# Up-projections of two batches cut into quarters, gates into halves, and a new order table: attention followed by a gated channel mix on one core

## The chip, the cores and the metric

The kernel runs on one core of one Trainium2 chip. The metric is device microseconds for one execution of the whole program. The engines are TensorE (PE), VectorE (DVE), ScalarE (ACT), GpSimd (POOL) and SyncE (SP, which here only issues DMAs).

## The reference

Eight batches, eight heads, 576 positions, head size 64. A linear attention without a big score matrix feeds a channel mix:

```
q_s = softmax(q, over d);  k_s = softmax(k, over positions)
kv  = k_s^T v                     # 64x64 per head
x   = q_s kv                      # joined over heads: (8, 576, 512)
xp  = x shifted by one position (0 in front)
xk  = mu_k*x + (1-mu_k)*xp;  xr = mu_r*x + (1-mu_r)*xp
k   = relu(xk @ w_k)              # 512 -> 1024
out = sigmoid(xr @ w_r) * ((k*k) @ w_v)
```

Inputs and output are float32 in HBM; the products run in bf16.

## The kernel before

**Units.** A batch is handled in two units u of four heads. Position 9p+j of a batch sits on partition p of block j, so that a batch has nine blocks of 64 rows, and "shifted by one" is the block before. Two batches make a pair i, with nine output tiles m of 128 rows.

**Steps of a unit.** load q, k, v (SyncE); exp of q and of k (ScalarE, L332); cast_v to bf16 (L336); sum_q and scale_q on VectorE (L341, L346); q is turned, for batches 0 and 1 by TensorE (turn_q, L357, and evict_q), later by a DMA (dma_turn_q, L368); kv (36 small 64x64 products, L372). Then the batches part:

- Batches 0 and 1 (NM = 2) fold the mix into the weights: weigh_kv (VectorE, L388) makes four scaled copies of kv, and x_mixed (L398) makes xk (w=0) and xr (w=1) directly, in two column parts c (blocks 0 to 4 and 5 to 8, PARTS). So x_mixed(b,u,w,c) has 12 matmuls for c=0 and 8 for c=1. evict_mixed copies each to SBUF.
- Batches 2 to 7 make x (L424), then shift_x (ScalarE, L438) and mix_x (VectorE, L443) blend each row half h for w=0 and w=1.

**Steps of the mix.** up(b,f) (L450) makes 128 of the 1024 hidden units, eight matmuls: two column halves a by four groups ct of 128 channels. Channels 2u and 2u+1 come from unit u. relu (ScalarE), square of two f at once (VectorE or ScalarE). gate(i,m) (L471): four matmuls over ct, then tanh. down(i,m) (L487): eight matmuls, finish (VectorE, L494), store.

**Weights** come as float32 into buffers that the run needs later, and are cast once: w_k in two halves of four f (load_wk; cast_wk, eight steps on GpSimd, ScalarE or VectorE), w_r (two casts on GpSimd), w_v (load_wv in two halves into the place where w_k lay; four casts).

**PSUM.** Three tiles of two banks ("two": turn, kv, x, x_mixed, up) and two of one bank ("one": gate, down).

**Order.** All of it is a list of steps. The class Plan takes a table ORDER of step numbers; a letter behind a number names the engine where there is a choice (A ScalarE, D VectorE, G GpSimd). It works out a start time for each step from costs written in the code, hands out buffers by it and emits the steps in order of these start times. On each engine the instructions stand in the table's order, and each engine takes its own strictly in that order; SyncE's loads, turns and stores likewise. TensorE's first fifteen microseconds are filled up with idle products (warm).

At the end, a branch (part) chooses a general path when a check of the softmax sums fails; then only the last two downs, finishes and stores follow.

Of the kernel before, what the change touches and what calls it, by code (L numbers as in the profile page):

```python
# [21 lines left out]
7 0 2 8 1 76 3 80 81 4 9 10 96 11 5 100 78G 77 79A 82 85 83A 12 6 13 84A 97 14 101 86 87 28 102  # L22
103A 90 92 91A 104D 93A 98G 99G 19 105 94 95A 16G 88 17G 106 107 108 89A 27 109D 24 110 111A 29
23G 136 15A 114 18D 112 362 363 21G 115D 367 30 113D 31 365 360 22G 25 32 368 26 33 372 20A 37
34 40 366 361 377 375 140 141 116 378 364D 376 370 120 371 369D 121 142 119G 526 536 117 527
143D 138G 122 42 373 118D 537 39G 144D 124D 125 43 137 521 531 123D 139A 44 38G 126 127 130 131A
128 129A 145 146 147 134 41 135A 148 149A 532 150 151D 36G 374A 152 154 153D 385 387 155D 35D
386 382 397 522 379D 156 159 388 523 398 160 389A 158 524 528 380 173 176 177 174 46 161 529 383
381 45 157 390 391 178 530 538 190 539 395 162 132 533 396 163 399A 392 133A 164 393 561 193 166
534 165 384D 47 49 394D 562 541 48 175 167 168 542 169 179 55 180 551 50 546 194 195 552 535 181  # L30
170 547 186 187 172 171 188 182 51 563 183 564 548 556 184 207 412 413 191 192 185 210 417 189
402 418 403 415 410 540 211 241 565 405 209 416 549 411 407 212 208 419D 408 406 244 245 576 196
197 400 56 57 557 571 401 414D 577 213 198 409D 572 200 404D 214 558 199 202 203 201 543 215 559
544 204 206 205 52 216 581 566 582 217 219 53 54 567 220 221 224 218 225 525 222 227 223 568 578
427 432 428 242 550 569 430 243 431 433 420 421 247 226 230 434A 586 246 437 228 248 438 587 579
422 423 58 231 249 254 255 424D 256 59 229 570 583 250 257 560 251 584 545 553 258 253 232 554
61 237 66 252 234 573 574 233 591 64 238 425 606 236 60 426 259 235 63 239 260 435 240 277 261
65 607 452 436 442 447 439D 429D 596 453 262 592 443 440 575 448 275 445 294 450 292 446 278 608
62 279 580 441 295 449D 451 597 293 263 455 264 280 298 598 444A 454A 609 601 299 456 276 265
599 266 600 602 267 268 281 282 270 555 611 612 67 588 269 68 272 621 283 589 271 274 622 273  # L40
285 284 593 73 289 594 69 626 286 610 288 627 457 616 458 603 459A 296 290 287 343 309 460 74
291 467 461 468 462 463 346 465 311 470 472 466 297 312 477 310 313 471 344 75 604 469D 590 628
478 345 473 300 585 314 617 347 71 315 618 302 595 629 316 641 301 305 619 304 464A 306 475 308
646 642 647 630 613 476 307 303 348 474A 317 323 479D 322 349 614 350 620 636 637 319 638 643
324 318 320 485 321 487 488 72 328 644 651 325 652 486 70 497 639 640 498 489D 492 326 329 490
493 327 495 496 482 483 330 491 499D 623 351 332 357 624 661 353 615 653 333 480 356 662 331
494D 481 358 654 352 656 657 631 632 359 484D 334 625 633 340 335 336 355 673 655 339 634 648
337 354 341 517 342 518 338 505 649 666 510 645 650 667 704 671 506 705 511 672 507 681 674 706
707 682 512 635 500 508 509A 513 515 675 676 514D 658 659 677 516 502 501 503 504D 660 519D 668
669 605 670 663 664 665 683 684 678 679 691 685 686 692 696 687 688 697 680 708 520 689 690 701  # L50
702 693 694 703 695 698 699 700
# [3 lines left out]
class Plan:  # L55
# [7 lines left out]
    TURN = 0.2  # L63
# [7 lines left out]
    def step(self, eng, cost, fn=None, after=(), uses=(), lat=0.12, narrow=False):  # L71
        s = {"eng": eng if isinstance(eng, dict) else {eng: cost}, "fn": fn, "lat": lat,
             "n": len(self.steps), "prev": [], "uses": [], "tail": False, "narrow": narrow}
        self.steps.append(s)
        self.link(s, after, uses)
        return s
# [7 lines left out]
    def run(self):  # L84

        busy, narrow, order = {e: 0.0 for e in ENGINES}, False, []
        for word in ORDER.split():
# [24 lines left out]
        return sorted(order, key=lambda s: s["start"])  # L112
# [30 lines left out]
def kernel(  # L143
# [18 lines left out]
    J = S // 64  # L162
# [123 lines left out]
    def wk_raw():  # L286
        return f32(at("k2", "w"), CT * F).rearrange("p (c a f) -> p a c f", a=2, c=CT)
# [162 lines left out]
    def up(b, f):  # L450
        ps, xk = at("two", "up", b, f), at("xk", b)
        for a in range(2):
            for ct in range(CT):
                nc.tensor.matmul(ps[:, a, 0:HS], lhsT=wk_bf[:, ct, 128 * f:128 * f + 128],  # L454
                                 rhs=xk[:, ct, HS * a:HS * a + HS], start=(ct == 0),
                                 stop=(ct == CT - 1))
# [14 lines left out]
    def gate(i, m):  # L471
        for ct in range(CT):
# [66 lines left out]
    T_UP, T_GATE, T_DOWN, T_NARROW = 0.98, 0.863, 1.725, 0.5  # L539
# [30 lines left out]
    for a in range(2):  # L570
        queue.append(dma(2.85, lambda a=a: load_wk(a), after=early[-1:], uses=[sl("k2", "w")]))
        for c in range(4):
            ev["wk", 4 * a + c] = pl.step(
                {"POOL": 0.65, "ACT": 0.58, "DVE": 0.6}, 0,
                lambda e, f=4 * a + c: cast_wk(e, f), after=[queue[-1]], uses=[sl("k2", "w")])
    queue.append(dma(2.85, load_wr, after=early[-1:], uses=[sl("xr", "w")]))
    ev["wr"] = [pl.step("POOL", 1.05, lambda c=c: cast_wr("POOL", c), after=[queue[-1]],
                        uses=[sl("xr", "w")]) for c in range(2)]
# [3 lines left out]
    for a in range(2):  # L582
        first.append(dma(2.75, lambda a=a: load_wv(a), uses=[sl("k2", "w")],
                         after=[*queue, *(ev["wk", i] for i in range(FT))]))
        for c in (2 * a, 2 * a + 1):
            ev["wv"].append(pl.step({"POOL": 1.2, "ACT": 1.05, "DVE": 0.9}, 0,
                                    lambda e, c=c: cast_wv(e, c), after=[first[-1]],
                                    uses=[sl("k2", "w")]))
# [4 lines left out]

    for n in range(B):
        for u in range(2):
# [5 lines left out]
            if n < NM:  # L601
# [3 lines left out]
                                     ev["ld", "v", n, u]], uses=[vb, sl("ldv", n, u)])  # L605
                      for h in range(2)]
            else:
                vc = [pl.step("POOL", 1.3, lambda n=n, u=u: cast_v("POOL", n, u),
                              after=[ev["ld", "v", n, u]], uses=[vb, sl("ldv", n, u)])]
            p = pl.step("DVE", 1.57, lambda n=n, u=u: sum_q(n, u), after=[qe], uses=[eq])  # L610
            p = pl.step("DVE", 1.32, lambda n=n, u=u: scale_q(n, u), after=[p], uses=[eq, qs])
# [13 lines left out]
            if n < NM:  # L625
                km = sl("kvm", n, u)
                nk = [p, ev["mu"]]
                for w in range(2):
                    nk.append(pl.step("DVE", 0.75 - 0.2 * w, lambda n=n, u=u, w=w: weigh_kv(n, u, w),
                                      after=nk, uses=[s, km, sl("mub")], lat=0.18))  # L630
                for w in range(2):
                    for c in range(2):
                        s = sl("two", "xm", n, u, w, c)
                        p = pl.step("PE", 0.47 if c == 0 else 0.41,
                                    lambda n=n, u=u, w=w, c=c: x_mixed(n, u, w, c),
                                    after=[nk[2 + w], *T], uses=[qT, km, s], lat=0.3, narrow=True)
# [6 lines left out]
            nk = pl.step("DVE", 0.42, lambda n=n, u=u: norm_kv(n, u), after=[p], uses=[s, kn],  # L643
                         lat=0.35)
            ss = [sl("two", "x", n, u, h) for h in range(2)]
            p = pl.step("PE", T_NARROW, lambda n=n, u=u: x(n, u), after=[nk, *T],
# [13 lines left out]
    for b in range(B):  # L660
        mixed = [ev["mix", b, u, 0, c] for u in range(2) for c in range(2)]
        relus = []
        for f in range(FT):
            s, r = sl("two", "up", b, f), sl("rel", b, f // 2)
            ev["up", b, f] = pl.step("PE", T_UP, lambda b=b, f=f: up(b, f),
                                     after=[ev["wk", f], *mixed], uses=[sl("xk", b), s], lat=0.2)
            relus.append(pl.step("ACT", 0.54, lambda b=b, f=f: relu(b, f),
                                 after=[ev["up", b, f]], uses=[s, r], lat=0.2))
            if f % 2:
# [3 lines left out]
                                              lat=0.2)  # L673
                relus = []
    for s in (ev["prep"], ev["up", 0, 0]):
        pl.link(s, [], [sl("one", "warm")])
    branch = pl.step("PE", 0.3, lambda: part())
    branch["tail"] = "first"
    for i in range(B // 2):
        for m in range(J):  # L680
            bs = [b for b in (2 * i, 2 * i + 1) if (m <= 4 if b == 2 * i else m >= 4)]
            s, th, ot = sl("one", "rp", i, m), sl("th", i, m), sl(kept(i, m), i, m)
            p = pl.step("PE", T_GATE, lambda i=i, m=m: gate(i, m),
                        after=[*ev["wr"], *(ev["mix", b, u, 1, c] for b in bs for u in range(2)
                                            for c in range(2))],
                        uses=[sl("xr", i), s, th], lat=0.2)
# [146 lines left out]
```

## Time and profile before

| | |
|---|---|
| median of 3 runs | 199.39 us (198.61 to 199.65) |
| the profiled execution | 199.28 us, span in the profile 197.5 us |
| granted TensorE clock, mean | 0.989 |
| busy: PE, DVE, ACT, POOL | 186.5, 145.6, 144.7, 30.4 us |
| read from and written to HBM | 33.56 and 9.44 MB |

A line of a timeline reads: start in us, length in us, engine, line of the kernel, operation, output <- input by tile names, shape, how many instructions the line merges, and in brackets the idle time just before it and what ended it. "PE two L454 <- POOL wk_bf L238: 0.9, 1, 0.9" in the list of waits: instructions of line 454 waited for a GpSimd cast of wk_bf, 0.9 us in total, once, longest 0.9. L238 and L237 are the copy helper (VectorE or GpSimd, and ScalarE). The busy digits are tenths in 40 equal slices of the span.

### The profile page before, as it was taken

How to read it: one execution, taken by the hardware profiler on the slowest of the kernel's cores; microseconds unless marked ns; L12 is line 12 of the kernel's file. 1: busy time of each engine (PE TensorE's matmuls, PEld its weight loads, DVE VectorE, ACT ScalarE, POOL GpSimd, SP SyncE). 2: the span in 40 equal slices, each digit the busy share in tenths (PEclk: the TensorE clock that was granted, in tenths of full speed). 3: DMA queues.
4: the chain of work that ended last, by engine and by line, in shares of the span. 5: the costliest groups of instructions: out<-in, count | busy, mean ns of one | idle time of the engine just before them, and what ended most of it. 6: DMA issues, size and time to landing. Idle time of an engine off the chain costs nothing. (4 is left out here: it accounts for less than half of the span.)

```text
span 197.5 us, 4726 instructions
## 1 busy us (share of the span) xinstructions
PE 186.5 (94%) x1903; PEld 111.4 (56%) x1903; DVE 145.6 (74%) x225; ACT 144.7 (73%) x212; POOL 30.4 (15%) x42
## 2 busy tenths in 40 slices
PE   6699899899999999999998999999999999999991
PEld 4366665655547754664675545755476546664441
DVE  1979896797899799948999779887658859126222
ACT  3898688799797986989769988998749591671210
POOL 2042763420120222000080000230200000000000
PEclk9879999999999999999999999999999999999998
DMA  5999999989999999869993499999622540515634
GB/s 207 371 399 386 389 390 386 389 314 240 276 388 205 229 397 294 272 61 278 403 399 87 86 250 359 318 229 276 236 51 59 113 106 10 124 30 124 162 72 127
DMA packets 35896, 46.86 MB, mean 237 GB/s; under 512 B 16280, under 2 KB 16544, under 8 KB 35872
## 3 DMA queue, kind: packets, MB, share of 16 engines
q1 hardware_dynamic: 35456, 46.02, 77.7%
q10 hardware_dynamic: 416, 0.53, 1.0%
q8 instruction: 15, 0.25, 0.5%
q14 instruction: 9, 0.07, 0.1%
HBM read 33.56 MB, written 9.44 MB: 218 GB/s over the span
## 5 line engine op out<-in xcount | busy, mean ns | idle before, releaser
L454 PE MATMUL two<-xk,wk_bf 128*128 128x288 bf16 x512 | 66.8, 286 | 1.2 <-POOL wk_bf L238 0.9
L490 PE MATMUL one<-wv_bf,k 128*128 128x512 bf16 (+1 forms) x296 | 66.2, 374 | 0.1
L454 PEld LDWEIGHTS <-wk_bf 128*128 128x128 bf16 x512 | 49.8, 98 | 18.1 <-POOL wk_bf L238 1.2
L459 ACT ACTIVATE rel<-two 128x576 bf16<-128x576 f32 x64 | 39.9, 650 | 20.3 <-PE two L454 17.0
L490 PEld LDWEIGHTS <-k 128*128 128x128 bf16 x296 | 28.1, 98 | 31.2 <-issue 0.8
L473 PE MATMUL one<-wr_bf,xr 128*128 128x512 bf16 x144 | 35.8, 379 | 0.0
L238 POOL CAST vb<-ldv 128x1152 bf16<-128x1152 f32 (+1 forms) x17 | 19.2, 1132 | 102.0 <-DMA ldv<-in_v_dram 94.0
L440 ACT ACTIVATE aw<-two,om 128x575 bf16<-128x575 f32 x48 | 32.6, 752 | 2.5 <-PE two L432 2.5
L478 ACT ACTIVATE th<-one 128x512 f32<-128x512 f32 x36 | 21.4, 603 | 13.5 <-PE one L473 13.4
L496 DVE SCALAR_TENSOR_TENSOR ot<-th,one 128x512 f32<-128x512 f32 x33 | 22.4, 681 | 11.9 <-PE one L490 9.1
L469 DVE TENSOR_TENSOR k<-rel 128x1152 bf16<-128x1152 bf16 x22 | 18.6, 860 | 11.3 <-ACT rel L459 11.2
L342 DVE TENSOR_REDUCE rs<-eq 128x18 f32<-128x1152 bf16 x16 | 21.6, 1348 | 3.4 <-ACT eq L332 3.3
L347 DVE TENSOR_TENSOR qs<-eq,inv 128x1152 bf16<-128x1152 bf16 x16 | 23.7, 1484 | 0.3
L445 DVE SCALAR_TENSOR_TENSOR xk<-two,mu,aw 128x576 bf16<-128x576 f32 x24 | 19.1, 812 | 3.3 <-ACT aw L440 3.3
L332 ACT ACTIVATE eq<-ldq 128x1152 bf16<-128x1152 f32 x16 | 18.5, 1170 | 3.2 <-DMA ldq<-in_q_dram 3.0
L473 PEld LDWEIGHTS <-xr 128*128 128x128 bf16 x144 | 13.4, 98 | 13.1 <-issue 0.2
L445 DVE SCALAR_TENSOR_TENSOR xr<-two,mu,aw 128x576 bf16<-128x576 f32 x24 | 19.1, 803 | 1.1 <-ACT aw L440 1.0
L332 ACT ACTIVATE ek<-ldk 128x1152 bf16<-128x1152 f32 x16 | 18.7, 1171 | 0.5 <-DMA ldk<-in_k_dram 0.5
L467 ACT ACTIVATE k<-rel 128x1152 bf16<-128x1152 bf16 x10 | 11.6, 1171 | 0.2
L378 PE MATMUL two<-vb,ek 64*64 64x65 bf16 x576 | 7.9, 197 | 1.0 <-ACT ek L332 0.5
L378 PEld LDWEIGHTS <-ek 64*64 64x64 bf16 x576 | 6.4, 110 | 3.9 <-ACT ek L332 0.9
L320 PE MATMUL one<-ident 128*128 128x256 bf16 x29 | 6.6, 387 | 1.8 <-DVE halves L258 1.8
(56 smaller groups left out, 86.0 us busy)
## 6 DMA issues: line engine op xcount, KB each, us to landing
ldq<-in_q_dram SPq DMA_DIRECT2D x16, 576.0 KB, 5.9
ldk<-in_k_dram SPq DMA_DIRECT2D x16, 576.0 KB, 8.4
out_dram<-ot SPq DMA_DIRECT2D x66, 128.0 KB, 2.5
ldv<-in_v_dram SPq DMA_DIRECT2D x14, 576.0 KB, 7.7
k<-in_moe_w_k_dram SPq DMA_DIRECT2D x2, 1024.0 KB, 12.6
k<-in_moe_w_v_dram SPq DMA_DIRECT2D x2, 1024.0 KB, 11.0
ldv<-in_v_dram SPq DMA_DIRECT2D x4, 288.0 KB, 10.5
xr<-in_moe_w_r_dram SPq DMA_DIRECT2D x1, 1024.0 KB, 13.1
```

What stands on the lines that cost most here:

```text
L238: return {"DVE": nc.vector, "POOL": nc.gpsimd}[eng].tensor_copy(out=out, in_=in_)
L332: nc.scalar.activation(out=at("e" + n, b, u)[:].rearrange("p j (h d) -> p h j d", h=2), in_=at("ld" + n, b, u)[:].rearrange("p h (j d) -> ...
L342: nc.vector.reduce_sum(out=rs[:], in_=at("eq", b, u)[:].rearrange("p j (h d) -> p (j h) d", h=2), axis=AX.X)
L347: nc.vector.tensor_tensor(out=at("qs", b, u)[:].rearrange("p j (h d) -> p (j h) d", h=2), in0=at("eq", b, u)[:].rearrange("p j (h d) -> p ...
L440: nc.scalar.activation(out=at("aw", b, u, h, w)[:, 1:S], in_=x_of(b, u, h)[:, 1:S], func=ACT.Copy, scale=om[:, c:c + 1])
L445: nc.vector.scalar_tensor_tensor(out=blend(b, w)[:, 2 * u + h, :], in0=x_of(b, u, h)[:, 64:64 + S], scalar=mu[:, c:c + 1], in1=at("aw", b, ...
L454: nc.tensor.matmul(ps[:, a, 0:HS], lhsT=wk_bf[:, ct, 128 * f:128 * f + 128], rhs=xk[:, ct, HS * a:HS * a + HS], start=(ct == 0), stop=(ct ...
L459: nc.scalar.activation(out=at("rel", b, f // 2)[:, f % 2, :].rearrange("p (a c) -> p a c", a=2), in_=at("two", "up", b, f)[:, :, 0:HS], fu ...
L473: nc.tensor.matmul(at("one", "rp", i, m)[:], lhsT=at("xr", i)[:, ct, 128 * m:128 * m + 128], rhs=wr_bf[:, ct, :], start=(ct == 0), stop=(c ...
L478: nc.scalar.activation(out=at("th", i, m)[:], in_=at("one", "rp", i, m)[:], func=ACT.Tanh, scale=0.5)
L490: nc.tensor.matmul(at("one", "vp", i, m, a)[:, cols], lhsT=at("k2", i)[:, f, 128 * m:128 * m + 128], rhs=wv_bf[:, f, cols], start=(f == 0) ...
L496: nc.vector.scalar_tensor_tensor(out=at(kept(i, m), i, m)[:, cols], in0=at("th", i, m)[:, cols], scalar=1.0, in1=at("one", "vp", i, m, a)[ ...
```

## The change

up gets the column halves and the units that it is to do, and gate the units:

```diff
-    def up(b, f):
+    def up(b, f, parts=(0, 1), us=(0, 1)):
         ps, xk = at("two", "up", b, f), at("xk", b)
-        for a in range(2):
-            for ct in range(CT):
+        for a in parts:
+            for ct in range(2 * us[0], 2 * us[-1] + 2):
...
-    def gate(i, m):
-        for ct in range(CT):
+    def gate(i, m, us=(0, 1)):
+        for ct in range(2 * us[0], 2 * us[-1] + 2):
```

In batches 0 and 1 an up becomes four steps, (a,u) for a and u in 0, 1, of two matmuls each; the quarter of u=0 opens the sum and that of u=1 closes it. A quarter of u=0 can run before unit 1's xk is there. Gates of pair 0 with m >= 4 become two steps by unit. The float32 place of w_k is laid out so that each half is contiguous:

```diff
-        return f32(at("k2", "w"), CT * F).rearrange("p (c a f) -> p a c f", a=2, c=CT)
+        return f32(at("k2", "w"), CT * F).rearrange("p (a c f) -> p a c f", a=2, c=CT)
```

The plan's clockwork learns that some steps of VectorE and GpSimd hold each other up (casts, scale_q, squares), and some costs are new:

```diff
-    TURN = 0.2
+    TURN, SHARE = 0.25, 0.7
...
+            if s["shares"] and e in sharing:
+                a, b = sharing["POOL" if e == "DVE" else "DVE"]
+                cost += self.SHARE * max(0.0, min(b, t + cost) - max(a, t))
+                sharing[e] = t, t + cost
...
-    T_UP, T_GATE, T_DOWN, T_NARROW = 0.98, 0.863, 1.725, 0.5
+    T_UP, T_GATE, T_DOWN, T_NARROW = 0.98, 0.863, 1.725, 0.55
...
-                    p = pl.step("PE", 0.47 if c == 0 else 0.41,
+                    p = pl.step("PE", 0.65 if c == 0 else 0.52,
```

These numbers act only through the emission's order. The number of matmuls, copies, loads and stores is the same. The table ORDER is new throughout. Read out of it, by step names:

```
TensorE, batch 0, before
  x_mixed(0,0,*) kv(0,1) x_mixed(0,1,*), all eight | up 1 3 2 0 | up 5 7 6 4 | turn_q(1,1) | gate 1 3
  turn_q(1,0) kv(1,0) gate 0 2
after
  six x_mixed and kv(0,1) | quarters of up 1 0 3 2 | x_mixed(0,1,1,0) x_mixed(0,1,1,1)
  quarters of up 4 5 6 7, turn_q(1,1) inside the last | gate 1 3 | turn_q(1,0) kv(1,0) gate 0 2
TensorE, batch 1, before
  seven x_mixed and kv(1,1) | up 2 3 1 7 | down 0 1 | up 0 4 | down 3 | up 6 | kv(2,0) x_mixed(1,0,1,0)
  down 2 | up 5 | x(2,0) gate 8 4 kv(2,1) gate 6 5 x(2,1) down 8 5 gate 7 | ups of batch 2
after
  six x_mixed and kv(1,1) | quarters of up 4 7 5 6 0 2 1 3 | down 3 1 | x_mixed(1,1,1,0) kv(2,0)
  x_mixed(1,1,1,1) | down 0 2 | x(2,0) kv(2,1) halves of gate 8 4 5 6 x(2,1) down 8 5 | gate 7 | ups of batch 2
cast_wk   before: GpSimd 1 2 7 5 6, ScalarE 0 4, VectorE 3
          after:  GpSimd 1 7 5, VectorE 0 3 2 4 6
cast_wr   both: GpSimd; the halves 0 1 before, 1 0 after
evict_mixed of batch 1   before: ScalarE 5, VectorE 3; after: ScalarE 8
between the last x of batch b and its first up, before
  b=3 gate gate down down | b=4 down gate up gate up | b=5 down gate up gate down | b=6 kv gate down down
after
  b=3 kv gate down down   | b=4 gate down up gate    | b=5 down up down gate      | b=6 down down gate
```

The last steps on TensorE are down(3,6), the branch, and then, before, down(3,8) first half, down(3,7), down(3,8) second half; after, down(3,7), down(3,8) in two halves.

More of the change, by code (lines that the diff above doesn't have):

```diff
@@ L28 @@
[L28 to L33, printed above, removed]
@@ new lines @@
+14 87 104A 28 88 16G 89D 103A 19 23G 94 95A 105 90 91A 27 106 92 93A 108 107 109A 110 111A 15D
+18D 365 24 367 366 360 21G 378 29 361 26 136 17D 368 379 369 362 376 377 373 363 380 374 364 140
+371 372 20D 30 22D 112 25 31 114 375 382 33 115A 383 384 119G 385 113D 387 393 389 395 139G 388
+116 386 390 396 394 32 391 141 398 37 399 370A 117 397 142 120 138G 121 400 144D 401 574 402
+143D 584 585 575 122 118D 125 569 123A 579 137 124D 126 127 580 128 145 146 147 134 129A 135A
+132 133A 148 149A 130 392D 131A 150 426 427 151A 442 443 34 444 445 40 381A 35D 446 431 433 428
@@ new lines @@
+192 454 56 464 599 196 625 212 197 583 629 630 213 462D 198 467D 592 200 214 199 455 201 610 243
+593 202 203 204 206 205 53 456 611 242 457D 634 215 247 245 635 248 216 619 217 218 221 620 58
+220 621 222 600 631 223 52 224 468 469 612 225 478 219 227 228 54 226 470 246 632 479 471 472D
+258 475 476 480 481 639 640 230 249 65 254 255 622 644 229 231 473 474 256 250 633 645 251 60
+482D 257 594 604 252 293 66 485 636 623 253 486 232 238 605 659 637 626 237 59 660 261 234 233
+239 61 483 484 477A 240 654 235 236 495 496 627 259 262 490 487D 649 275 650 491 62 488 493 489
@@ new lines @@
+317 322 323 324 318 319 676 326 677 696 699 320 538 325 321 539 543 347 545 700 697 546 540 530
+541 678 544 668 709 710 348 542D 531 329 330 533 704 705 528 529 689 690 691 331 534 692 351 357
+332 352 356 706 547D 693 333 707 532A 358 535 714 359 536 715 724 673 353 334 537D 716 717 725
+355 339 340 711 718 712 336 341 701 726 354 335 337 563 564 338 558 702 553 559 554 555 713 708
+556 565 727 342 757 728 758 759 550 566 557A 567A 719 734 698 735 760 720 548 551 560 549 729
+552D 561 562D 721 703 722 730 723 736 737 731 686 732 738 739 687 733 744 740 749 745 741 750
@@ L69, in slot, with step @@
         return {"kind": kind, "users": 0, "idx": None, "end": 0.0}
-    def step(self, eng, cost, fn=None, after=(), uses=(), lat=0.12, narrow=False):
+    def step(self, eng, cost, fn=None, after=(), uses=(), lat=0.12, narrow=False, shares=False):
         s = {"eng": eng if isinstance(eng, dict) else {eng: cost}, "fn": fn, "lat": lat,
-             "n": len(self.steps), "prev": [], "uses": [], "tail": False, "narrow": narrow}
+             "n": len(self.steps), "prev": [], "uses": [], "tail": False, "narrow": narrow, "shares": shares}
         self.steps.append(s)
@@ L86, in run @@
         busy, narrow, order = {e: 0.0 for e in ENGINES}, False, []
+        sharing = {"DVE": (0.0, 0.0), "POOL": (0.0, 0.0)}
         for word in ORDER.split():
@@ L574 @@
                 {"POOL": 0.65, "ACT": 0.58, "DVE": 0.6}, 0,
-                lambda e, f=4 * a + c: cast_wk(e, f), after=[queue[-1]], uses=[sl("k2", "w")])
+                lambda e, f=4 * a + c: cast_wk(e, f), after=[queue[-1]], uses=[sl("k2", "w")],
+                shares=True)
     queue.append(dma(2.85, load_wr, after=early[-1:], uses=[sl("xr", "w")]))
     ev["wr"] = [pl.step("POOL", 1.05, lambda c=c: cast_wr("POOL", c), after=[queue[-1]],
-                        uses=[sl("xr", "w")]) for c in range(2)]
+                        uses=[sl("xr", "w")], shares=True) for c in range(2)]
     first = [ld(n, 1, u, early[-1:]) for n, u in (("q", 0), ("q", 1), ("k", 0), ("v", 0), ("k", 1))]
@@ L592 @@
                 ld(n, b, u, first)
+    weighed: list = []
     for n in range(B):
@@ L608 @@
                 vc = [pl.step("POOL", 1.3, lambda n=n, u=u: cast_v("POOL", n, u),
-                              after=[ev["ld", "v", n, u]], uses=[vb, sl("ldv", n, u)])]
+                              after=[ev["ld", "v", n, u]], uses=[vb, sl("ldv", n, u)],
+                              shares=True)]
             p = pl.step("DVE", 1.57, lambda n=n, u=u: sum_q(n, u), after=[qe], uses=[eq])
-            p = pl.step("DVE", 1.32, lambda n=n, u=u: scale_q(n, u), after=[p], uses=[eq, qs])
+            p = pl.step("DVE", 1.32, lambda n=n, u=u: scale_q(n, u), after=[p], uses=[eq, qs],
+                        shares=True)
             if n < NM:
@@ L633 @@
                         s = sl("two", "xm", n, u, w, c)
-                        p = pl.step("PE", 0.47 if c == 0 else 0.41,
+                        p = pl.step("PE", 0.65 if c == 0 else 0.52,
                                     lambda n=n, u=u, w=w, c=c: x_mixed(n, u, w, c),
-                                    after=[nk[2 + w], *T], uses=[qT, km, s], lat=0.3, narrow=True)
+                                    after=[nk[2 + w], *T], uses=[qT, km, s], lat=0.25, narrow=True)
                         ev["mix", n, u, w, c] = pl.step(
@@ L642 @@
             kn = sl("kvs", n, u)
-            nk = pl.step("DVE", 0.42, lambda n=n, u=u: norm_kv(n, u), after=[p], uses=[s, kn],
-                         lat=0.35)
+            nk = pl.step("DVE", 0.42, lambda n=n, u=u: norm_kv(n, u), after=[p],
+                         uses=[s, kn], lat=0.35)
             ss = [sl("two", "x", n, u, h) for h in range(2)]
-            p = pl.step("PE", T_NARROW, lambda n=n, u=u: x(n, u), after=[nk, *T],
+            p = pl.step("PE", T_NARROW, lambda n=n, u=u: x(n, u), after=[nk, *T, *weighed],
                         uses=[qT, kn, *ss], lat=0.3, narrow=True)
@@ L660 @@
     for b in range(B):
-        mixed = [ev["mix", b, u, 0, c] for u in range(2) for c in range(2)]
         relus = []
         for f in range(FT):
-            s, r = sl("two", "up", b, f), sl("rel", b, f // 2)
-            ev["up", b, f] = pl.step("PE", T_UP, lambda b=b, f=f: up(b, f),
-                                     after=[ev["wk", f], *mixed], uses=[sl("xk", b), s], lat=0.2)
+            s, r, both = sl("two", "up", b, f), sl("rel", b, f // 2), []
+            whole = ((0, 1), (0, 1), 0.2)
+            for a, us, lat in (whole,) if b >= NM else [
+                    ((a,), (u,), 0.2 * u) for a in range(2) for u in range(2)]:
+                ev["up", b, f] = pl.step(
+                    "PE", T_UP * len(a) * len(us) / 4,
+                    lambda b=b, f=f, a=a, us=us: up(b, f, a, us),
+                    after=[ev["wk", f], *(ev["mix", b, u, 0, c] for u in us for c in range(2)
+                                          if c in a or c == 0 or b >= NM),
+                           *(both[-1:] if us == (1,) else ())],
+                    uses=[sl("xk", b), s], lat=lat)
+                both.append(ev["up", b, f])
             relus.append(pl.step("ACT", 0.54, lambda b=b, f=f: relu(b, f),
-                                 after=[ev["up", b, f]], uses=[s, r], lat=0.2))
+                                 after=both, uses=[s, r], lat=0.2))
             if f % 2:
@@ L676, with needs @@
         pl.link(s, [], [sl("one", "warm")])
+    def needs(b, m, c):
+        lo, n = PARTS[c]
+        return b >= NM or any(lo <= blk - J * (b % 2) < lo + n for blk in (2 * m, 2 * m + 1))
     branch = pl.step("PE", 0.3, lambda: part())
@@ L682 @@
             s, th, ot = sl("one", "rp", i, m), sl("th", i, m), sl(kept(i, m), i, m)
[L683 to L686, printed above, removed]
+            p = None
+            for us in ((0, 1),) if i or m < 4 else ((0,), (1,)):
+                p = pl.step("PE", T_GATE * len(us) / 2, lambda i=i, m=m, us=us: gate(i, m, us),
+                            after=[*ev["wr"], *(ev["mix", b, u, 1, c] for b in bs for u in us
+                                                for c in range(2) if needs(b, m, c)),
+                                   *([p] if p else ())],
+                            uses=[sl("xr", i), s, th], lat=0.2 if us[-1] else 0.0)
             t = pl.step("ACT", 0.49, lambda i=i, m=m: tanh(i, m), after=[p], uses=[s, th],
```

46 lines of the change are left out of this document (19 added, 27 removed).

## The prediction

> **What bounds the kernel now.** I read the page first, then the waits of TensorE, then the timeline of the two stretches that the change rewrites (16 to 40 us, and the ups that open each later batch), and last the chain that ends the run.
>
> ```profile
> span 197.5 us, 4726 instructions
> PE 186.5 (94%) x1903; PEld 111.4 (56%) x1903; DVE 145.6 (74%) x225; ACT 144.7 (73%) x212; POOL 30.4 (15%) x42
> ...
> PE   6699899899999999999998999999999999999991
> ...
> GB/s 207 371 399 386 389 390 386 389 314 240 276 388 205 229 397 294 272 61 278 403 399 87 86 250 359 318 229 276 236 51 59 113 106 10 124 30 124 162 72 127
> ```
>
> A slice is 4.94 us. From the ninth slice to the last but one TensorE is full; DMA moves 371 to 399 GB/s in the second to eighth slice. So there are two regimes: up to 40 us bytes are owed, after that TensorE's own work is the time. What TensorE waited for:
>
> ```profile
> PE two L361 <- DVE qs L347: 1.5, 1, 1.5
> PE two L454 <- POOL wk_bf L238: 0.9, 1, 0.9
> PE two L378 <- ACT ek L332: 0.5, 1, 0.5
> PE two L410 <- ACT xk L237: 0.4, 2, 0.3
> ```
>
> Only the third lies behind 40 us. An edit of order can win the few waits of the head, that 0.5, and no more; the end (last down at 193.45, finish, store, 4.05 us) is the same work in both tables. The stretch with the largest wait that the change touches:
>
> ```profile
> 17.56 2.62 PE L454 MATMUL two<-xk,wk_bf 128*128 128x288 bf16 x20
> ...
> 20.19 3.41 POOL L238 CAST wk_bf<-k 128x512 bf16<-128x512 f32 x3 [3.02 <-DMA k<-in_moe_w_k_dram]
> ...
> 20.37 1.64 DVE L347 TENSOR_TENSOR qs<-eq,inv 128x1152 bf16<-128x1152 bf16 x1
> ...
> 22.54 4.09 PE L454 MATMUL two<-xk,wk_bf 128*128 128x288 bf16 x32 [0.89 <-POOL wk_bf L238]
> ...
> 24.43 2.55 POOL L238 CAST wr_bf<-xr 128x1024 bf16<-128x1024 f32 x2 [0.83 <-DMA xr<-in_moe_w_r_dram]
> ...
> 26.98 1.89 PE L473 MATMUL one<-wr_bf,xr 128*128 128x512 bf16 x8
> ```
>
> Four ups run on the first half of w_k, then TensorE stands 0.89 us for GpSimd's casts of the second half. The first gate begins at 26.98, the moment wr's cast ends (24.43 + 2.55).
>
> **Part 1, batch 0 (16 to 29 us).** The change splits an up into four quarters of two matmuls: the same 8 matmuls in all, 4.09/32 = 0.128 us each, nothing added. It puts two of the mixed products (20 matmuls, about 0.8 us by the starts 16.31 to 17.16 to 17.56) behind the first four ups, and gives VectorE five of the eight w_k casts (before: one), ScalarE none (before: two). The first half's cast of f=1 is there at 16.6 (16.00 + 0.61), and the quarters of unit 0 need only unit 0's evictions, so ups start about 16.7 rather than 17.56. Four ups, 4.05, give 20.75; the two products 21.55. The second half lands at 20.19; casts of 0.61 (GpSimd) and 0.43 (VectorE), one after the other 7, 4, 5, 6, end at 20.8, 21.2, 21.8 and 22.2; up 4 wants its cast at 21.55, ups 5 and 6 at 22.6. The 0.89 wait is covered. Four ups and turn_q (0.6) end at 26.2, against 26.98 with the same work done.
>
> What is late next: wr. Its landing (24.43) is bound by bytes and moves with nothing here; two casts of 1.04 alone end at 26.5, so gates start 0.45 earlier at most. And behind them kv(1,0) needs a half of v that VectorE casts last: scale_q(1,0) after the lock 26.5 to 27.85, two evictions 0.42 each, cast 0.66: 29.35, so kv(1,0) at 29.4, where before it ran at 29.45. The gain of this part, 0.45 to 0.8, is given back there: I take 0, and keep 0 to 0.45.
>
> The casts are put one after the other because GpSimd's and VectorE's shared steps exclude each other in the rows: a w_k cast takes 613 ns alone and 1738 ns beside scale_q,
>
> ```profile
> L238 POOL CAST wk_bf<-k x5: 613/613/1738, 16.0 to 22.4; 128x512 bf16<-128x512 f32 x5
> ```
>
> and wr's second cast took 1.56 instead of 1.04 behind a square. The 1738 ns cast was queued at 20.8 and ran when scale_q ended at 22.01: it stood still for the rest of it, and did not run slower. The Trainium skill, SBUF — State Buffer, section "SBUF: two separate sides", speaks against the change here: the port pair that the two engines share is an exclusive lock, held for a whole instruction by whichever came first. The trace agrees (1.13 us of standing still). By that rule a scale_q(1,0) that starts just ahead of wr's second cast would hold all gates back by its whole 1.34 us, and the total below would be -0.3; if the two only slowed each other, as 1.56 for 1.04 might be read, it would stay -1.1. Whose turn comes first is rival 2.
>
> The new layout of w_k's raw half (contiguous per half) frees load_wv from the other half's casts: SyncE's 2.7 us wait there (issue at 23.63) shrinks to about 22.2. The queue in front was not empty (388 GB/s between 16 and 27), so 0, at most nothing gained or lost.
>
> **Part 2, batch 1 (29.4 to 40 us).** Before, seven mixed products and kv run from 31.70 to 35.29 with small waits (0.42, 0.43, 0.27, 0.34 in the loads' and matmuls' rows), and the first up starts at 35.64. After, six products stand ahead of the ups instead of seven. All six evictions are on ScalarE, start to start 0.59 and 0.48: first at 32.15, the fourth done at 34.45, which frees the two-bank tile of up 4: ups from 34.55. That is 1.1 earlier, less one product (0.45) still owed: 0.65. ScalarE then owes a square 1.07, eight relus 0.53, four exps 1.07, a tanh 0.48 up to 45.7; the ups need their tiles at 40.45 (relu 0 done 39.7) and 40.9 (relu 6 done 40.25): no wait, with 0.65 to spare. Take -0.65; ends 0 (ScalarE's ops at full duration, 0.1 more each, use the spare) and -1.65 (gates at 26.5 and no wait until the fourth up).
>
> **Part 3, the rest.** kv(6,0) waited 0.51 at 108.60 for its exp; the table puts that exp some 15 ScalarE steps earlier: -0.5 (ends 0 and -0.5). A narrow step (64-row products) between wide ones costs more than one beside another narrow one: kv and x alone take 0.41 + 0.40 (starts 53.50 to 53.91, 51.27 to 51.67), together 0.69 (70.65 to 71.34), and the up ahead of one 1.07 against 0.98. Behind 40 us the new order has 15 such groups for 17: 0.1 to 0.2 each, -0.3. Halved gates add no instruction. New waits in 150 us of other order: before had one of 0.5; bounds 0 and 1.0, I take +0.35.
>
> Sum: -0.65 - 0.5 - 0.3 + 0.35 = **-1.1 us**. The profiled execution took 199.28 us (span 197.5 and 1.78 around it): 198.2; it stood 0.11 under the median of 199.39: 198.3.
>
> **Rivals.** (1) *Bytes hold the head*: part 2's lead is lost to v and k of batch 1 as part 1's is to wr. For it: 388 GB/s up to 40 us. Against: the waits of 31.7 to 35.6 name evictions, not DMA. Then -0.45, 198.9. (2) *The lock falls the other way*: scale_q(1,0) starts before 25.42 and wr's second cast waits 1.34. Gates at 27.85, kv(1,0) at 30.2 instead of 29.45: -1.1 + 0.8, 199.1. I have the scale ready at 25.85, 0.4 on the good side. (3) *Slower: the blends of batches 3 to 6 come late.* The first up of a batch waits for the last xk blend on VectorE. Before, it had little to spare:
>
> ```profile
> 79.47 0.82 DVE L445 SCALAR_TENSOR_TENSOR xk<-two,mu,aw 128x576 bf16<-128x576 f32 x1 [0.21 <-ACT aw L440]
> ...
> 80.56 1.63 PE L454 MATMUL two<-xk,wk_bf 128*128 128x288 bf16 x12
> ```
>
> 80.29 against 80.56: 0.27, and by the same reading 0.6, 0.8 and 0.5 in batches 4 to 6. TensorE's work between the batch's last x and its first up (gate 0.87, down 1.73, up 0.98, kv 0.4) shrinks from 5.2, 5.43, 6.18, 4.73 to 4.73, 4.45, 5.31, 4.33: by 0.47, 0.98, 0.87, 0.40. If blends come as long after x as before: waits of 0.2, 0.4, 0.1, 0 = 0.7. If each comes 0.5 later (one tanh ahead on ScalarE): 0.70 + 0.88 + 0.57 + 0.40 = 2.55, and the time is 199.39 - 1.45 + 2.55 = 200.5. It makes the kernel slower from some 0.2 later on, where these waits reach 1.45. Against it: the new order puts both xk blends of the last unit ahead of an xr one in most of these batches. (4) *The split gives nothing and nothing else moves*: quarters are worth no time where ups wait for casts and tiles, as in part 1; inside 198.9 to 199.4.
>
> **How the numbers follow.** Half a per cent, 1.0 us, is about what a measurement of this kernel can tell (its three runs span 1.04). Forecast 0.56, of which 0.44 is over 0.5% faster; rivals 1 and 4 0.16, nearly all within; rival 2 0.09, of which 0.05 within (what is later behind it decides); rival 3 0.16, slower; 0.03 for a full win of all waits (-1.65 - 0.5 - 0.4 = -2.5, 196.9). Faster 0.47, same 0.33, slower 0.20. The range runs from that full win, 196.9, to rival 3's 200.5; the forecast's own is 197.3 to 199.0.
>
> **What would show it.** Right: no wait of an up on wk_bf; gates first at 26.5 to 27.0; batch 1's first up at 34.3 to 34.9; kv(6,0) unwaited; TensorE's last down at about 192.4. Wrong: the first gate later than 27.5 (rival 2); batch 1's ups at 35.5 (rival 1); waits of L454 on VectorE's L445 behind 70 us (rival 3).

## The result and the profile after

The changed kernel takes 198.68 us (median of 22 runs, 196.69 to 199.88), the kernel before 199.60 in the same series (22 runs, 198.61 to 200.60). The ratio is 0.9946, 95% interval 0.9925 to 0.9966: about 1.1 us faster. Runs that took over 1.5% more than the fastest of the same kernel are left out of this ratio and of those below: one here, one of after_again, two of scale_late. The profiled execution took 198.17 us with a span of 196.3, before 199.28 and 197.5. The total came out as forecast, but its parts did not.

The page of the changed kernel, span, busy times and TensorE's slices:

```profile
span 196.3 us, 4719 instructions
...
PE 186.9 (95%) x1904; PEld 111.7 (57%) x1904; DVE 143.6 (73%) x224; ACT 145.6 (74%) x214; POOL 30.1 (15%) x41
...
PE   6989969999999999999999999999999999999992
```

TensorE's busy time is the same within 0.4 us (186.9, before 186.5); its idle time fell from 11.0 to 9.4 us. Its waits, in the order engine, tile and line that waited, what it waited for, total, times, longest:

```profile
PE one L481 <- POOL wr_bf L246: 1.6, 1, 1.6
PE two L369 <- DVE qs L355: 0.7, 1, 0.7
PE two L418 <- ACT xk L245: 0.3, 1, 0.3
PE one L498 <- DVE ot L504: 0.3, 1, 0.3
PE two L462 <- ACT xk L245: 0.2, 1, 0.2
```

(Lines have moved by 8 to 10: up L462, gate L481, down L498, kv L386, scale_q L355, the copy helper L246 and L245.) The waits on wk_bf and on the exp of k(6,0) are gone, as forecast. A new one of 1.6 us, the largest in the part that the change rewrites, stands ahead of the first gate. The timeline shows how it came about:

```profile
16.75 4.09 PE L462 MATMUL two<-xk,wk_bf 128*128 128x288 bf16 x32
...
20.38 1.18 DVE L246 CAST wk_bf<-k 128x512 bf16<-128x512 f32 x2
20.41 1.62 POOL L246 CAST wk_bf<-k 128x512 bf16<-128x512 f32 x2 [3.73 <-DMA k<-in_moe_w_k_dram]
...
22.21 1.34 DVE L355 TENSOR_TENSOR qs<-eq,inv 128x1152 bf16<-128x1152 bf16 x1
...
23.47 1.34 DVE L350 TENSOR_REDUCE rs<-eq 128x18 f32<-128x1152 bf16 x1
...
24.61 3.15 POOL L246 CAST wr_bf<-xr 128x1024 bf16<-128x1024 f32 x2 [2.58 <-DMA xr<-in_moe_w_r_dram]
...
25.14 1.71 DVE L355 TENSOR_TENSOR qs<-eq,inv 128x1152 bf16<-128x1152 bf16 x1
...
27.81 1.89 PE L481 MATMUL one<-wr_bf,xr 128*128 128x512 bf16 x8 [1.64 <-POOL wr_bf L246]
...
35.56 8.00 PE L462 MATMUL two<-xk,wk_bf 128*128 128x288 bf16 x64 [0.18 <-ACT xk L245]
```

TensorE begins its ups at 16.75 and is ready for the gates at about 26.2. But scale_q(1,0) on VectorE starts at 25.14, while w_r's first cast runs on GpSimd, and gets its turn before the second one. The two casts, 1.04 us each alone, take 3.15, and the first gate runs at 27.81. Batch 1's first up comes at 35.56, before 35.64: nothing is won by then. The gain lies later. From 100 to 125 us (columns: window, length, busy time of PE, PEld, DVE, ACT, POOL, granted clock, DMA share, GB/s), the kernel before and then the one after:

```profile
100.00:125.00 25.00, 24.36 (x264) 14.08 (x263) 21.71 (x29) 21.90 (x31) 3.92 (x4) 1.00 0.77 238
```

```profile
100.00:125.00 25.00, 25.00 (x277) 15.39 (x276) 20.83 (x30) 19.66 (x30) 3.53 (x2) 1.00 0.96 282
```

The starts of single steps, read off TensorE's weight loads (a few matmul records are missing, loads hardly ever), cut the span into three. "Last" is down(3,8) second half; "body" reaches from batch 2's first up to it, "tail" from there to the span's end. (after_again and late_again are experiments below.)

| kernel | up(0) | kv(1,0) | up(1) | up(2) | body | tail | span |
|---|---|---|---|---|---|---|---|
| before | 17.55 | 29.36 | 35.23 | 60.26 | 131.92 | 5.30 | 197.48 |
| after | 16.75 | 30.12 | 35.31 | 60.57 | 130.71 | 5.00 | 196.28 |
| after_again | 16.70 | 31.48 | 37.14 | 62.07 | 130.70 | 5.01 | 197.78 |
| late_again | 17.70 | 29.60 | 34.82 | 59.74 | 130.70 | 5.04 | 195.48 |

So the change is +0.31 in the head, -1.22 in the body and -0.30 in the tail: -1.21. The head differs from execution to execution of the same kernel. The body of the new table hardly does; the old table's was 131.92 here and 132.37 in before_tail (below), where the exp of k(6,0) held TensorE 0.9 us instead of 0.5.

What TensorE did in the body (columns as above), before and then after:

```profile
60.26:192.18 131.92, 131.13 (x1215) 76.65 (x1214) 96.12 (x140) 95.23 (x142) 12.15 (x9) 1.00 0.71 195
```

```profile
60.57:191.28 130.71, 130.56 (x1216) 76.59 (x1215) 95.35 (x143) 93.98 (x140) 13.22 (x10) 1.00 0.74 205
```

So of the 1.22, 0.64 is idle time (0.79 before, 0.15 after) and 0.57 is busy time, for the same matmuls.

### The profile page after: what moved, and what is told of

The parts are those of the page before. It is cut to its first block, busy times and chain, and to the rows that moved or that the text cites. A ratio compares the mean times of both kernels' runs of the same rounds, so it can differ in the third digit from the quotient of the medians.

```text
span 196.3 us, 4719 instructions
## 1 busy us (share of the span) xinstructions
PE 186.9 (95%) x1904; PEld 111.7 (57%) x1904; DVE 143.6 (73%) x224; ACT 145.6 (74%) x214; POOL 30.1 (15%) x41
## 5 line engine op out<-in xcount | busy, mean ns | idle before, releaser
L462 PE MATMUL two<-xk,wk_bf 128*128 128x288 bf16 x512 | 66.8, 286 | 0.3 <-ACT xk L245 0.2
L498 PE MATMUL one<-wv_bf,k 128*128 128x512 bf16 (+1 forms) x296 | 66.3, 373 | 0.4 <-DVE ot L504 0.3
L462 PEld LDWEIGHTS <-wk_bf 128*128 128x128 bf16 x512 | 49.9, 98 | 17.0 <-issue 0.6
L498 PEld LDWEIGHTS <-k 128*128 128x128 bf16 x296 | 28.2, 98 | 31.3 <-issue 1.2
L481 PE MATMUL one<-wr_bf,xr 128*128 128x512 bf16 x144 | 35.5, 379 | 1.6 <-POOL wr_bf L246 1.6
L246 POOL CAST vb<-ldv 128x1152 bf16<-128x1152 f32 (+1 forms) x18 | 19.6, 1090 | 91.0 <-DMA ldv<-in_v_dram 73.5
L477 DVE TENSOR_TENSOR k<-rel 128x1152 bf16<-128x1152 bf16 x23 | 19.4, 854 | 10.9 <-ACT rel L467 10.9
L355 DVE TENSOR_TENSOR qs<-eq,inv 128x1152 bf16<-128x1152 bf16 x16 | 23.3, 1454 | 0.3
L481 PEld LDWEIGHTS <-xr 128*128 128x128 bf16 x144 | 13.5, 98 | 15.3 <-issue 2.0
L475 ACT ACTIVATE k<-rel 128x1152 bf16<-128x1152 bf16 x9 | 10.4, 1170 | 0.0
L386 PE MATMUL two<-vb,ek 64*64 64x65 bf16 x576 | 7.6, 194 | 0.1
L386 PEld LDWEIGHTS <-ek 64*64 64x64 bf16 x576 | 6.1, 107 | 2.4 <-ACT rel L467 0.9
```

Of the source, the lines that this page charges most:

```text
L246: return {"DVE": nc.vector, "POOL": nc.gpsimd}[eng].tensor_copy(out=out, in_=in_)
L355: nc.vector.tensor_tensor(out=at("qs", b, u)[:].rearrange("p j (h d) -> p (j h) d", h=2), in0=at("eq", b, u)[:].rearrange("p j (h d) -> p ...
L481: nc.tensor.matmul(at("one", "rp", i, m)[:], lhsT=at("xr", i)[:, ct, 128 * m:128 * m + 128], rhs=wr_bf[:, ct, :], start=(ct == 0), stop=(c ...
L498: nc.tensor.matmul(at("one", "vp", i, m, a)[:, cols], lhsT=at("k2", i)[:, f, 128 * m:128 * m + 128], rhs=wv_bf[:, f, cols], start=(f == 0) ...
```

## Experiments

Step numbers of ORDER are given with the step's name.

**after_again**: the changed kernel, unchanged, as measure for the next three.

> The changed kernel itself, as the base on this chip for the three variants beside it. Both theories: 0.994 of the kernel before. In the profile the first gate near 27.8 us (waiting for w_r's cast), batch 1's first up near 35.6.

Measured: 199.03 us (12 runs, 196.85 to 200.67), ratio 0.9959 (0.9927 to 0.9992). The profiled execution took 199.58: TensorE stood 1.98 us ahead of the first gate, and what followed ran on a slower clock (last column but two):

```profile
28.10 2.49 PE L481 MATMUL one<-wr_bf,xr 128*128 128x512 bf16 x8 [1.98 <-POOL wr_bf L246]
```

```profile
28.00:30.00 2.00, 1.90 (x8) 0.78 (x8) 0.64 (x1) 0.62 (x2) 0.68 (x2) 0.81 1.05 392
30.00:32.00 2.00, 2.00 (x47) 1.53 (x45) 0.41 (x1) 1.08 (x2) 1.35 (x2) 0.50 1.04 386
32.00:34.00 2.00, 2.00 (x24) 0.82 (x12) 1.31 (x6) 1.76 (x2) 0.00 (x0) 0.84 1.05 390
```

The first gate is 0.29 later than in the other profile of the same kernel, and batch 1's first up 1.83 later. The other 1.5 us is the clock at 0.50 from about 29.3 to 32.7.

**scale_late**: scale_q(1,0) is put behind the two evictions that have to wait for TensorE's turn_q(1,1), so that it normally comes after w_r's second cast.

```diff
-138G 121 400 144D 401 574 402 143D
+138G 400 144D 401 574 402 143D 121      # 121 scale_q(1,0), 143D evict_q(1,1,0)
```

> The changed kernel with scale_q(1,0) put behind the two evictions of turn_q(1,1) in VectorE's order, so that it starts after w_r's second cast has taken the shared port. Theory (the head's gain was lost to that lock, rival 2 of the prediction): w_r's second cast ends near 26.7 instead of 27.8, first gate at 26.8, kv(1,0) at 29.1 instead of 30.1, batch 1's first up near 34.6 instead of 35.6, time 0.7 to 1.0 us under the changed kernel. Rival (bytes hold the head): the gate comes earlier as well, but kv(1,1) waits for v and the first up stays at 35.3 or later; time within 0.3 us of the changed kernel.

Measured: ratio 0.9881 (0.9857 to 0.9905), from five runs of 196.46 to 197.13; that is 1.6 us under after_again, where 0.7 to 1.0 was expected. Two other runs took 200.52 and 200.58. The profiled execution is the first of these two, and it shows that the move does not settle the turn: w_r's first cast could start only at 25.62, a microsecond later than in the profile after, scale_q was ready at 26.27, during that cast, and got its turn before the second one again. The casts were 1040 and 2162 ns. TensorE stood 2.9 us, and the eight matmuls of the first gates took 3.25 us instead of 1.89. Of the other run there is no trace.

```profile
L246 POOL CAST wr_bf<-xr x2: 1040/1601/2162, 25.6 to 26.6; 128x1024 bf16<-128x1024 f32 x2
```

```profile
25.62 3.15 POOL L246 CAST wr_bf<-xr 128x1024 bf16<-128x1024 f32 x2 [3.37 <-DMA xr<-in_moe_w_r_dram]
...
26.27 1.59 DVE L355 TENSOR_TENSOR qs<-eq,inv 128x1152 bf16<-128x1152 bf16 x1
...
28.81 3.25 PE L481 MATMUL one<-wr_bf,xr 128*128 128x512 bf16 x8 [2.90 <-POOL wr_bf L246]
```

**whole_b0** and **whole_b01**: the ups of batch 0, then of batches 0 and 1, whole again, each at the place of its last quarter.

```diff
-                    lambda b=b, f=f, a=a, us=us: up(b, f, a, us),
+                    lambda b=b, f=f, a=a, us=us: up_last(b, f) if b < NM else up(b, f, a, us),
```

up_last emits nothing in the first three calls and the whole up in the fourth (b == 0 in whole_b0).

> The changed kernel with batch 0's ups whole again, each put where its last quarter stood; all else the same. Theory (batch 0's quarters win nothing, since w_r holds the gates): the first up at 17.6 instead of 16.75, the last up still done before 27, the first gate at 27.8, time within 0.2 us of the changed kernel. Rival (the quarters are where the gain comes from): the 0.8 us of the start goes through to the end, +0.8 us.

> As before, with batch 1's ups whole as well. Theory: the first whole up of batch 1 must wait for the last of the six evictions on ScalarE, near 36.5 instead of 35.6, and nothing behind gives it back: +0.9 us over the changed kernel, about level with the kernel before. Rival (quarters worth nothing in both batches): within 0.2 us of the changed kernel.

Measured: whole_b0 197.84 us, ratio 0.9934 (0.9910 to 0.9958); whole_b01 198.84, 0.9981 (0.9953 to 1.0008). Batch 0's quarters are worth nothing that can be seen. One expectation missed: with whole ups the first up of whole_b0 began at 16.64, not at 17.6.

```profile
16.64 4.24 PE L462 MATMUL two<-xk,wk_bf 128*128 128x288 bf16 x32
```

whole_b01 is 0.4 us over after_again, where 0.9 was expected, and the intervals overlap. In its profile scale_q stayed behind the casts (1040 and 1042 ns), and a wait of 0.7 us appeared at batch 1's first up on the eviction of xk. Its loss to whole_b0 mixes the two; late_whole below separates them.

**late_finish**: scale_late, and also finish(0,3) ahead of scale_q(2,1), to free down(0,0)'s tile before the new wait on ot.

```diff
-413 176 576 175 177 161
+413 176 576 175 587 177 161      # 587 finish(0,3), 177 scale_q(2,1)
```

> The changed kernel with scale_q(1,0) behind the two evictions, and finish(0,3) ahead of scale_q(2,1), since down(0,0) waited for its bank near 48 us. Theory: w_r's second cast ends one microsecond earlier when the first lands near 24.6, batch 1's ups start near 34.6, and the wait of 0.3 at down(0,0) is gone: 0.985 to 0.988 of the kernel before. Rival (the first edit's gain of the last comparison was the chip's mood): 0.994.

Measured: 196.93 us (6 runs, 196.43 to 197.19), ratio 0.988 (0.9852 to 0.9908). The wait of L498 on ot is gone from its list, w_r's casts took 1040 ns each, the first gate ran at 26.7, batch 1's first up at 34.23. In time it can't be told from scale_late.

**before_exp**, **before_tail**, **before_exp_tail**: two single features of the new table, put into the old one.

```diff
-451 597 293                  # before_exp: 293 exp k(6,0), 451 relu(4,4)
+293 451 597
...
+276 444A                     # 276 exp k(5,1) ahead of 444A square(4,1)
...
-701 702 693 694 703 695 698 699 700
+693 694 695 701 702 703 698 699 700   # before_tail: store(3,7) first, then both halves of m=8
```

> The kernel before with two exps of keys moved forward in ScalarE's order: exp k(6,0) ahead of relu(4,4), exp k(5,1) ahead of square(4,1). Theory (behind 40 us the change won by not waiting for these exps): the waits of kv(6,0) and kv(5,1) near 108 and 112 us are gone, 0.6 to 0.9 us under the kernel before. Rival (such a wait only moves to the relus and squares behind): within 0.2 us of the kernel before.

> The kernel before with the tail of the change: down(3,7) ahead of the two halves of down(3,8), and finishes and stores in that order. Theory (the last store no longer stands behind another's issue on ScalarE's queue): from the start of the last down to the end 4.75 us instead of 5.09, 0.3 us under the kernel before. Rival (the difference was chance of that one profile): 5.1 us and no change of time.

> Both edits in the kernel before: no quarters, no halves, the old table otherwise. Theory: 0.9 to 1.2 us under the kernel before, level with the changed kernel, which then owes its gain to these places and nothing to the quarters. Rival (the quarters carry the gain): at most 0.4 us under the kernel before.

Measured: before_exp 1.0006 (0.9983 to 1.0029), before_tail 0.9985 (0.9963 to 1.0008), before_exp_tail 0.9999 (0.9976 to 1.0022). In the profiles the stretch from batch 4's first up to batch 5's shrank from 24.68 to 24.10 in both with the exps moved, and the tail from 5.30 to 5.01 and 5.02 with the stores moved. The times don't show it. In these profiles batch 2 began up to 1.0 later (61.31 and 60.84 in the two with the exps moved, 60.26 before) with a longer wait on w_k's casts (1.5 and 1.2 us, before 0.9). Why the old table gave nothing back stays open: the old head varies by as much as was looked for, so I asked the same of a kernel whose times lie closer together.

**late_exp_back**: late_finish, with both exps moved back behind relu(4,4).

```diff
+499 293 276                  # 499 relu(4,4); 293 and 276 taken from their earlier places
```

> The table of late_finish with the exp of k(6,0) and the exp of k(5,1) moved back behind relu(4,4) on ScalarE, where the table before had them. Theory (the waits at kv(6,0) and kv(5,1) were real time, and before_exp did not show it because the head of the kernel before varies by more than this): 0.5 to 0.9 us over late_finish, about 197.6, ratio 0.9915, and the profile shows a wait of PE on ScalarE's exp at the line of kv near 105 us. Rival (what waits there is made up later, as before_exp's time says): as late_finish, about 196.9, ratio 0.988.

Measured: 198.60 us, ratio 0.9951 (0.9923 to 0.9979), against 0.9855 (0.9825 to 0.9885) for late_again on the same chip: 1.8 us slower, twice what I had expected. The timeline (late_exp_back, then late_again at the same place):

```profile
108.50 0.48 PE L386 MATMUL two<-vb,ek 64*64 64x65 bf16 x36
...
109.24 2.23 ACT L340 ACTIVATE ek<-ldk 128x1152 bf16<-128x1152 f32 x2
...
110.47 0.48 PE L386 MATMUL two<-vb,ek 64*64 64x65 bf16 x36 [1.49 <-ACT ek L340]
```

```profile
105.11 1.19 ACT L340 ACTIVATE ek<-ldk 128x1152 bf16<-128x1152 f32 x1
...
107.69 0.81 PE L386 MATMUL two<-vb,ek 64*64 64x65 bf16 x72
```

kv(6,0) stands 1.49 for its exp, and batch 4's first up to batch 5's takes 23.77 instead of 22.12. This wait is paid in full at the end: nothing behind 40 us makes up for it.

**late_tail_back**: late_finish with the old order of the last downs and stores.

```diff
-746 747 754 748 755 756 751 752 753
+754 755 746 747 756 748 751 752 753   # 754 down(3,8) first half, 746 down(3,7), 748 store(3,7)
```

> The table of late_finish with the order of the last three downs and stores as before: down(3,8,1), down(3,7), store(3,8,1), store(3,7), down(3,8,0). Theory (the store of (3,7) standing just ahead of the last store cost 0.3 us): about 197.2, ratio 0.9895, and last down to the end of the span 5.3 us. Rival (the tail's order costs nothing): 196.9, ratio 0.988, and 5.0 us.

Measured: 197.56 us, ratio 0.9898 (0.9866 to 0.9929). The tail is 5.30, with the new order 5.04; the body is as in late_again (130.61 and 130.70), the head 0.4 shorter. The intervals overlap, so the time does not tell the two apart; the 0.26 is the profile's. The last stores are issued in part by SyncE and in part by ScalarE. The issues of both queues (start, and length from the first issue to the end of the last), late_tail_back's and then late_again's:

```profile
188.30 4.15 ACTq L514 DMA_DIRECT2D out_dram<-last  x5
...
189.12 3.04 SPq L514 DMA_DIRECT2D out_dram<-last  x3
```

```profile
188.72 3.99 ACTq L514 DMA_DIRECT2D out_dram<-last  x5
...
190.66 2.01 SPq L514 DMA_DIRECT2D out_dram<-last  x3
```

Counted from the last down's first weight load (189.92 and 190.44), SyncE's issues end after 2.24 and 2.23 us, ScalarE's after 2.53 and 2.27. So the 0.26 stands in ScalarE's queue. Its last issue takes 0.80 us with the old order and 0.50 with the new; in the new order one of 0.78 is the last but one. This fits what was expected of before_tail, an issue that stands behind another's; no run tests that alone.

**late_whole**: late_finish with all ups of batches 0 and 1 whole (the edit of whole_b01).

> The table of late_finish with the ups of batches 0 and 1 whole again, each at the place of its last quarter. It measures the split of the change by itself, with the lock on the port out of the way in both. Theory (the quarters of batch 1 are worth the wait on the xk copy, which was 0.7 us in whole_b01's list of waits, and those of batch 0 are worth nothing): 0.7 us over late_finish, about 197.6, ratio 0.9915, and the profile shows that wait ahead of batch 1's first up. Rival (the split is worth nothing, and whole_b01 lost to whole_b0 only by the lock): as late_finish, about 196.9, ratio 0.988.

Measured: 197.33 us, ratio 0.9894 (0.9853 to 0.9935), against 0.9855 for late_again; the intervals overlap. Its profile has the expected wait:

```profile
PE two L462 <- ACT xk L245: 0.7, 1, 0.7
```

With whole ups the first matmul of batch 1's first up runs at 35.64, with quarters at 35.07. These two starts are not on a par, since w_r's cast began 0.7 us later in late_whole (25.32 and 24.61). From batch 1's first weight load to batch 2's, where that falls out, it is 25.51 us with whole ups and 24.92 or 24.93 in all four profiles of this table with quarters. So the quarters of batch 1 save about 0.6 us, of which the medians show 0.5 and the ratios 0.8, within their uncertainty.

**late_again**: late_finish once more, as measure for these three.

> late_finish unchanged, as the measure for the three others on the same chip. Both theories: about 196.9 (196.4 to 197.2), ratio 0.988, first gate near 26.7 us, the weight's two casts 1.04 us each. If its times scatter by more than 1.5 us, the lock is not all that scatters the times of the new table.

Measured: 196.83 us (6 runs, 196.77 to 197.27), ratio 0.9855 (0.9825 to 0.9885). Its timeline at the gates:

```profile
24.61 2.03 POOL L246 CAST wr_bf<-xr 128x1024 bf16<-128x1024 f32 x2 [3.05 <-DMA xr<-in_moe_w_r_dram]
...
26.96 1.89 PE L481 MATMUL one<-wr_bf,xr 128*128 128x512 bf16 x7
...
27.48 1.35 DVE L355 TENSOR_TENSOR qs<-eq,inv 128x1152 bf16<-128x1152 bf16 x1
```

w_r's first cast starts at 24.61, to the hundredth as after the change, and the casts are done 1.12 earlier because scale_q runs at 27.48. This is the best version that was found: about 1.2% under the kernel before in one series, 1.45% in the other.

## Why the prediction was right, and where it was not

**Part 1, batch 0: the casts held, the order of turns did not.** Ups began at 16.75 (forecast 16.7) and none waited on wk_bf. The reason given for the early start, that a quarter of unit 0 needs only unit 0's evictions, is not needed: whole_b0's whole ups began at 16.64. What is left is the place of the two mixed products, behind the first ups. The step that failed is the one on the second half of w_k's casts. I let VectorE and GpSimd take strictly alternate turns, with VectorE's last cast done at 22.2. It was done at 21.56 (20.38 + 1.18), so scale_q(1,1), sum_q(1,0) and scale_q(1,0) followed one another without a gap from 22.21, and the last began at 25.14 instead of 25.85. The 0.4 us that I had put between my forecast and rival 2 was smaller than this error of 0.7.

**Rival 2 is what happened.** It had scale_q(1,0) ahead of w_r's second cast, the gates at 27.85 and kv(1,0) at 30.2; the profile has 27.81 and 30.12. scale_late, in its five faster runs, and late_finish take this turn away, and with it about 1.6 us by the ratios of one series (0.9959 to 0.9881). The exclusive lock of the Trainium skill (SBUF — State Buffer, "SBUF: two separate sides") is borne out: the second cast takes 2164 ns in the profile after and 1040 when scale_q comes later. Its price was under-estimated: I took the delay of kv(1,0), 0.8. In after_again the wait also cost the clock, 1.5 more. In the first series the changed kernel's runs lie between 196.7 and 199.9, those of late_finish and late_again between 196.4 and 197.3. The turn and the clock, which the profiles of after, after_again and scale_late show, need not be all of that spread: late_whole has the turn settled too, and lies between 197.16 and 199.15. In the profiles of the new table's kernels the first up began anywhere between 16.30 (late_tail_back) and 18.33 us (late_exp_back); why is open.

**Part 2, -0.65: not there after the change, there without rival 2.** Batch 1's first up was forecast at 34.55, and came at 35.56. With scale_q out of the way it began at 34.82 and 34.23 by its first weight load, before 35.23: 0.4 and 1.0 earlier in two profiles of one kernel. The sign named for rival 1 (bytes), ups at 35.5, did appear, but rival 2 gives it too, and the same two profiles rule rival 1 out: w_r, v and k come from the same queue at the same rate there (385 to 393 GB/s between 24 and 34 us), and the ups start earlier. The split by itself is worth some 0.6 us, all of it in batch 1.

**Part 3: right, and too small.** kv(6,0) no longer waits, and late_exp_back shows that this order is real time. The body is -1.22, where the -0.5 for the exp and -0.3 for the narrow groups make -0.8. The new wait that I had allowed 0.35 for came as 0.3 at down(0,0), on the finish that frees its tile, and lies in the head. Of the body's -1.22, idle time gave 0.64, where the exp was put at 0.5; 0.28 of the 0.79 before were gaps that the prediction did not count. Busy time gave 0.57. The narrow groups, put at 0.3, are the only reason named for that, and no run tests them by themselves. So an edit of order won more behind 40 us than "that 0.5, and no more": TensorE's own work was not fixed there.

**The tail** I had called the same work in both tables, and it is; but the order of the stores was not the same, and that is worth 0.26 to 0.30 in all profiles. This term was missing. TensorE's last down ended at 192.56, where about 192.4 was forecast.

**Rivals 3 and 4 fell.** L462 waits for nothing on VectorE in the list above, though TensorE's cover shrank as reckoned. And the split with the new table did move the time.

So the sum of -1.1 was right because errors cancelled: the head, with the new wait in it, was forecast at -0.30 and came at +0.31; the body made good 0.4 of that, and the tail 0.3. That the total fits to a tenth is luck.

## What to carry to other kernels

Two engines that lock each other out make an order of two steps a matter of a few tenths of a microsecond. If such a step stands ahead of everything, as w_r's cast does here, don't let its turn hang on a few tenths: a step in between that must wait settled it in the profiles of late_finish to late_again, but not in scale_late's, where the weight came a microsecond later. And don't forecast it by a margin that is smaller than the error of the chain in front. A wait in a full engine's body is paid in full: in the best table the places of two exps are worth 1.6 us of the body, the cutting of products 0.6. Where one kernel's runs scatter by more than the effect looked for, take the cause of the scatter away first and measure then.

## What was not expected of the hardware

A wait of TensorE can cost more than itself. After 1.98 us of standing still ahead of the first gate (after_again) the granted clock fell to 0.50 for about 3.5 us, after 2.90 us (scale_late) likewise; after 1.64 us (the profile after) it stayed at 1.00. The Trainium skill (TensorE: Matmul & The Clock Gate, "HAM oscillation — how this bites in real kernels") puts the idle gap that throttles at over some 3.4 us. These runs show less, and the length alone does not decide: in nine of the fourteen profiles the clock also fell to 0.50 at some point between 7.9 and 9.6 us, beside a gap of TensorE of only 1.20 to 1.79 us. In the kernel before, TensorE stood from 7.54 to 9.03 us (the rows below, columns as above), while a gap of 1.75 us in whole_b0, from 26.20 on, left the clock at 1.00. What decides is open.

```profile
8.00:8.50 0.50, 0.00 (x0) 0.00 (x0) 0.50 (x1) 0.45 (x2) 0.00 (x0) 1.00 1.01 378
8.50:9.00 0.50, 0.00 (x0) 0.00 (x0) 0.50 (x2) 0.26 (x1) 0.00 (x0) 0.73 0.99 373
9.00:9.50 0.50, 0.47 (x5) 0.48 (x6) 0.50 (x1) 0.50 (x1) 0.00 (x0) 0.50 1.05 410
```

The landing of w_r, on the same queue behind the same transfers, lay between 24.4 and 25.6 us in the profiles, read off the start of its first cast. So an order that rests on a landing is one that differs from execution to execution.
